# A fused attention and gated MLP block on one core: half-width GpSimd sums, a product sum built from PSUM alone, and weight words cut at other steps

## The chip, the cores and the metric

The kernel runs on one core of a Trainium2 chip. The metric is device time in microseconds (us) from launch to end; less is better. A measurement is the median of several runs; the profile is of one further execution with the hardware profiler on.

Engines are named as the profile names them: PE is TensorE's matmul, PEld its weight load, DVE is VectorE, ACT is ScalarE, POOL is GpSimd, SP is SyncE, which here only issues DMAs. Each engine works through its own queue in order, and waits at an instruction until the semaphores that it names have come.

## The reference

S = 2048 rows of D = 576 are normalized. One branch is linear attention with 32 heads, the other a gated MLP with Df = 4608; the result is x + s * silu(MLP). In the part that the change touches, all in float32:

```python
g = jnp.einsum("bsd,df->bsf", xn, w_gate)   # 2048x576 by 576x4608
u = jnp.einsum("bsd,df->bsf", xn, w_up)
h = _gelu(g) * u
mlp = jnp.einsum("bsf,fd->bsd", h, w_down)
```

## The kernel before

**Stages.** First attention's keys, values, queries and output, then (from 285 to 1123 us of the profile) the matrices of gate and up, last the down projection. The change lies in the third stage.

**Seven products instead of eight.** Each product of two matrices is cut into 2x2 blocks and computed with seven block products, from sums of blocks of X and of W. The stage runs 36 *matrices*, numbered q: q even is a gate, q odd the up matrix for the same 256 columns of Df (group g = q // 2 of NG = 18). A matrix has seven steps k, in each of which one word list of W meets one of X, for two halves s of the rows (s = 1 first):

```python
STEPS = (
    ("al", "A11", "B11"), ("ga", "S1", "T1"), ("de", "S3", "T3"), ("be", "S2", "T2"),
    ("al", "A12", "B21"), ("ga", "S4", "B22"), ("de", "A22", "T4"),
)
```

The first name is a pair of PSUM banks (one for each s). Steps 0 to 3 start banks, steps 4 to 6 accumulate into the banks of steps 0 to 2, and the next matrix takes the eight banks in rotation, so that each bank is taken up again four steps later. Between, its value must have been read; `step` in `matrix` (L882) says by whom.

**The matmuls.** A float32 operand is split into a high and a low float32r word, so a step has 27 matmuls of 32 rows by 512 columns for each s. TensorE is used as four groups of 32 rows, which run side by side, each some matmuls behind the one before it (`roll`, L828). All four are issued in one order: a matmul at the head that waits for a bank holds up all of them.

**The sum of products.** For each s, u holds al, the first product. The block C22 needs al + ga + de + be: ACT copies ga into a buffer (a gate uses the place in h where the result will be, an up matrix a temporary), DVE adds de, adds be to u, and adds u to the buffer. u, with be in it, then serves steps 5 and 6. A gate's four blocks pass through Gelu on ACT into h (`gate_matrix`, L911); an up matrix multiplies them into h on DVE (`up_matrix`, L934).

**Gated values.** The down projection is computed the same way, so at steps 5 and 6 of an up matrix POOL forms four sums and differences of blocks of h for each s (`hs`, 128x512), and SP stores h and hs: ten DMAs. For the last group DVE and POOL's DMA queue do it.

**Words of W.** `load_mat(q)` (L769) issues on SP the DMA of one matrix of W into `raw`, one buffer for even and odd alike. `mat_sums(q)` (L774) lets POOL form S1 to S4 from it into `sm`. `cut_w` (L786) cuts a block: ACT writes the high words, DVE two subtractions the low words, into `wa` (A11, S1, S3, S2) or `wb` (A12, A22, S4). `mat_pieces(q)` (L793) returns which of these cuts are made after which step of the matrix *before*: A11 after step 0, S1 and S3 after step 2, S2 after 3, A12 and A22 after 4, S4 after 6. `matrix_of(q)` (L1425) runs `mat_sums(q + 1)`, takes `mat_pieces(q + 1)` and adds to step 4 the load of matrix q + 2, which is allowed once A12 and A22 of q + 1 have been cut from `raw`. In a gate it also adds the load of a block of w_down (`td`) at step 0 and POOL's sums of it at step 3.

**Order.** All of this is pinned to program order, so the order in which the Python code calls `act`, `vec`, `pool` and `dma` is the order in each engine's queue. After the matmuls of a step and a half s follow the instructions of `step`; after the second half follow the pieces of that step.

Of the kernel before, what the change touches and what calls it, by code (L numbers as in the profile page):

```python
# [10 lines left out]
AF = mybir.ActivationFunctionType  # L11
# [4 lines left out]
P = 128  # L16
# [8 lines left out]
TBN = S // TB  # L25
TT = TBN // P
NG = DF // (2 * P)
# [38 lines left out]
def block_kernel(ctx, tc, x, xe, xt_d, wq_d, wkv0_d, wkv1_d, wkv2_d, wo, wgu_d, wd_d, out):  # L66
    nc = tc.nc
# [21 lines left out]
    def mid(i, shape, dt, name):  # L89
        return sb.tile(shape, dt, tag=f"m{i}", bufs=1, name=name)  # L90
# [7 lines left out]
    def tmp(shape, name):  # L98
        return sb.tile(shape, F32, tag="tmp", bufs=4, name=name)
# [3 lines left out]
    def act(*args, **kw):  # L103
        pin(nc.scalar.activation(*args, **kw))  # L104

    def vec(op, *args, **kw):
        pin(getattr(nc.vector, op)(*args, **kw))  # L107
# [6 lines left out]
    def pool(op, *args, **kw):  # L114
        pin(getattr(nc.gpsimd, op)(*args, **kw))  # L115

    def dma(out, in_, eng=None):
        tc.keep_in_program_order((eng or nc.sync).dma_start(out=out, in_=in_))
# [636 lines left out]
    raw, sums, wt = {}, {}, {}  # L755
# [30 lines left out]
    def cut_w(o, src, nm):  # L786

        r = group(W_LO[nm])
        act(o[:, :, 0:3, :], src, AF.Copy)
        vec("tensor_sub", o[:, :, 3:5, :], src[:, :, 0:2, :], o[:, :, 0:2, :].bitcast(F32))  # L790
        vec("tensor_sub", o[r, :, 2, :], src[r, :, 2, :], o[r, :, 2, :].bitcast(F32))

    def mat_pieces(q):  # L793

        if q >= NQ:
            return [[] for _ in range(7)]
        rv, sm = sums.pop(q)
        if q % 2 == 0:
            raws_ = [lambda: cut_w(wt["b"][:, 1:3], rv[:, 1], "A12")]
        else:  # L800
            raws_ = [
                lambda: cut_w(wt["b"][:, 1:2], rv[:, 1, 0:1], "A12"),
                lambda: cut_w(wt["b"][:, 0:1], rv[:, 1, 1:2], "A22"),
            ]
        return [
            [lambda: cut_w(wt["a"][:, 0:1], rv[:, 0, 0:1], "A11")],
            [],
            [lambda: cut_w(wt["a"][:, 1:3], sm[:, 0:2], "S1")],
            [lambda: cut_w(wt["a"][:, 3:4], sm[:, 2:3], "S2")],
            raws_,  # L810
            [],
            [lambda: cut_w(wt["b"][:, 3:4], sm[:, 3:4], "S4")],
        ]

    STEPS = (
        ("al", "A11", "B11"), ("ga", "S1", "T1"), ("de", "S3", "T3"), ("be", "S2", "T2"),
# [62 lines left out]
                        mats[q] = matrix_of(q)  # L879
                    mats[q](k, s, bs[q, bk, s])  # L880

    def matrix(q, c22, done, todo):  # L882

        u = {}

        def step(k, s, b):
            if k == 0:
                u[s] = tmp([P, TBN], f"u_{q}_{s}")
                act(u[s], b, AF.Copy)
            elif k == 1:  # L890
                act(c22(s), b, AF.Copy)
            elif k == 2:
                vec("tensor_add", c22(s), c22(s), b)
            elif k == 3:
                vec("tensor_add", u[s], u[s], b)
                vec("tensor_add", c22(s), c22(s), u[s])
                done(s, 1, 1, None)
            elif k == 4:
                done(s, 0, 0, b)
            elif k == 5:  # L900
                done(s, 0, 1, (u[s], b))
            else:
                done(s, 1, 0, (u[s], b))
            if s == SBS[-1]:
                run(todo[k])

        return step

    hid = {}

    def gate_matrix(g, todo):  # L911
        for s in SBS:
            for b in range(2):
                hid[s, b] = slot([P, 2, TBN], F32, f"h_{g}_{s}_{b}")

        def done(s, f, b, src):
            o = hid[s, b][:, f]
            if src is None:
                src = o
            elif isinstance(src, tuple):  # L920
                vec("tensor_add", o, *src)
                src = o
            act(o, src, AF.Gelu_apprx_tanh)

        return matrix(2 * g, lambda s: hid[s, 1][:, 1], done, todo)

# [5 lines left out]
    td_d = dr.tile([NG, P, 4, HALF], F32, name="td")  # L932

    def up_matrix(g, todo):  # L934
        c22, sm = {}, {}

        def take(s):
            if s not in c22:
                c22[s] = tmp([P, TBN], f"u22_{g}_{s}")
            return c22[s]  # L940

        def done(s, f, b, src):
            if src is None:
                src = c22[s]
            elif isinstance(src, tuple):
                o = src[0] if (f, b) == (1, 0) else tmp([P, TBN], f"u12_{g}_{s}")
                vec("tensor_add", o, *src)
                src = o
            h1, h2 = hid[s, 0], hid[s, 1]
            h = hid[s, b][:, f]  # L950
            vec("tensor_mul", h, h, src)
            d = hs_d[g][:, s]

            eng, sum_ = (nc.gpsimd, vec) if g == NG - 1 else (nc.sync, pool)
            if (f, b) == (0, 1):
                sm[s] = [gl_tile([P, TBN], f"hs_{g}_{s}_{i}") for i in range(3)]
                sum_("tensor_sub", sm[s][0], h1[:, 0], h2[:, 0])
                sum_("tensor_add", h2[:, 0], h2[:, 0], h2[:, 1])
                sum_("tensor_sub", sm[s][1], h2[:, 0], h1[:, 0])
                dma(out=d[:, 4], in_=sm[s][0], eng=eng)  # L960
                dma(out=d[:, 2:4], in_=h2, eng=eng)
            elif (f, b) == (1, 0):
                sum_("tensor_sub", sm[s][2], h1[:, 1], sm[s][1])
                dma(out=d[:, 0:2], in_=h1, eng=eng)
                dma(out=d[:, 5], in_=sm[s][1], eng=eng)
                dma(out=d[:, 6], in_=sm[s][2], eng=eng)

        return matrix(2 * g + 1, take, done, todo)

    td = {}  # L970

# [333 lines left out]
    for n in range(3, 2 * TT):  # L1305
# [8 lines left out]
        if TT <= n < 2 * TT - 1:  # L1314
            j, c = divmod(n - TT, 2)
# [98 lines left out]
    pieces = []  # L1414
# [3 lines left out]
            run(aside.get((tb, t), []))  # L1418
    wt["b"] = big(14, [P, 4, 5, P], F32R, "wb")
    back("T3")  # L1420
    run(pieces[4] + pieces[6])
    load_mat(1)
    back("B21", "B22", "T4", eng=nc.sync)

    def matrix_of(q):  # L1425

        g = q // 2
        mat_sums(q + 1)
        todo = mat_pieces(q + 1)
        if q % 2 == 0:  # L1430
            todo[0].append(lambda: load_down(g))
            todo[3].append(lambda: down_sums(g))
        todo[4].append(lambda: load_mat(q + 2))
# [69 lines left out]
```

## Time and profile before

| | us |
|---|---|
| median of three runs (1530.05, 1533.8, 1530.51) | 1530.51 |
| the profiled execution, whole | 1536.36 |
| its span, first to last instruction | 1534.6 |
| stage of gate and up matrices in it | 838 |
| one gate and one up matrix together (596.09 to 642.17) | 46.1 |
| busy in that pair: DVE | 35.9 |
| busy in that pair: POOL | 23.8 |
| busy in that pair: ACT | 15.4 |
| mean granted TensorE clock | 0.993 |

How to read the profile: the page's first part gives each engine's busy time. In the timeline a row has its start and length in us, the engine, the line of the helper that recorded it (L104 ACT, L107 DVE, L110 matmuls, L115 POOL, L118 DMAs), the operation, its tiles as out<-in with numbers left out, the form and count, and in brackets how long the engine stood idle before it and what ended that. Tile names carry the sense: `u<-al` is the copy of step 0, `wa<-raw` a cut of A11, `wa<-sm` of S1 and S3 or S2, `wb<-raw` of A12 and A22, `wb<-sm` of S4, `hs<-h` and `h<-h` on POOL the gated sums. A row of waits has who waited for whom, us in total, times, and the longest. Since the helpers have one line each, lines of code tell little here, tiles and times tell most.

### The profile page before, as it was taken

What the parts mean: (1) busy time and instruction counts of PE and PEld (TensorE: products, weight loads), DVE (VectorE), ACT (ScalarE), POOL (GpSimd) and SP (SyncE); (2) the same over time, 40 slices, a digit from 0 to 9 for tenths busy, and PEclk for the clock granted to TensorE, in tenths of its full rate; (3) what the DMA queues carried; (4) which work ended last, traced back from release to release, by engine and by line L of the source; (5) the groups of instructions that cost most, each with busy time, mean ns of one, the idle gap of its engine ahead of it and who ended that gap; (6) DMA issues with size and microseconds to landing.
All of it is one profiled execution on the core that took longest, in us unless ns stands there. A gap on an engine that the chain in (4) does not pass through costs nothing.

```text
span 1534.6 us, 42632 instructions
## 1 busy us (share of the span) xinstructions
PE 1489.4 (97%) x18431; PEld 1395.8 (91%) x18431; DVE 1074.2 (70%) x1651; ACT 614.6 (40%) x1155; POOL 548.0 (36%) x520
## 2 busy tenths in 40 slices
PE   9999999999999999999999999999999999999998
PEld 8989989998888988888988888988889999999998
DVE  7676567177788787788787787777684666555775
ACT  5444455233332333332333332333344545444543
POOL 5452521134655444655444655444510020000120
PEclk9999999899999999999999999999999999999999
DMA  6354015623443423443323443333687757787873
GB/s 231 128 217 165 1 52 193 247 79 129 169 170 135 148 100 129 170 169 134 150 99 129 170 170 134 139 110 129 221 285 246 253 167 251 245 267 246 281 243 127
DMA packets 114550, 261.98 MB, mean 171 GB/s; under 512 B 10218, under 2 KB 38634, under 8 KB 112314
## 3 DMA queue, kind: packets, MB, share of 16 engines
q1 hardware_dynamic: 112586, 249.95, 45.8%
q0 software_dynamic: 1632, 8.91, 1.6%
q8 instruction: 144, 2.36, 0.6%
q14 instruction: 44, 0.36, 0.1%
q10 hardware_dynamic: 144, 0.39, 0.1%
HBM read 161.27 MB, written 97.91 MB: 169 GB/s over the span
## 4 chain that ended last, share of the span: by engine, by line
PE 50%; issue 16%; DVE 14%; POOL 12%; DMA 4%; ACT 3%; POOLq 0%; ACTq 0%; SPq 0%; DVEq 0%
PE bd L1069 26%; PE kv L110 7%; POOL sm L115 5%; POOL hs L115 5%; DVE h L107 4%; PE de L110 4%; PE s L110 3%; DVE wa L107 3%; POOL h L115 3%; DVE u L107 3%; PE ga L110 3%; PE al L110 2%; DMA raw<-in_wgu_dram 2%; DVE wb L107 2%; PE q L110 2%
## 5 line engine op out<-in xcount | busy, mean ns | idle before, releaser
L1069 PE MATMUL bd<-t,s 128*128 128x288 f32 x3024 | 404.6, 296 | 2.4 <-DVE u L107 2.4
L1069 PEld LDWEIGHTS bd<-t,s 128*128 128x128 f32 x3024 | 403.8, 189 | 3.3 <-DVE u L107 2.9
L110 PE MATMUL al<-xo_B,wa 32*128 32x512 f32 x972 | 254.1, 394 | 14.3 <-DVE u L107 14.3
L107 DVE TENSOR_TENSOR s<-sr,s 128x512 fp32r<-128x512 f32 x252 | 176.0, 738 | 123.9 <-ACT s L104 120.2
L110 PE MATMUL ga<-xr_B,wb 32*128 32x512 f32 x972 | 253.5, 393 | 8.7 <-ACT h L104 8.6
L110 PE MATMUL ga<-xo_T,wa 32*128 32x512 f32 x972 | 253.8, 394 | 5.9 <-ACT h L104 5.9
L110 PE MATMUL de<-xo_T,wa 32*128 32x512 f32 x972 | 246.9, 389 | 5.5 <-DVE h L107 5.5
L110 PE MATMUL al<-xr_B,wb 32*128 32x512 f32 x972 | 252.1, 390 | 0.0
L110 PE MATMUL al<-xr_B,wa 32*128 32x512 f32 x972 | 251.7, 391 | 0.0
L110 PE MATMUL de<-xr_T,wb 32*128 32x512 f32 x972 | 250.5, 390 | 0.0
L110 PE MATMUL de<-xo_T,wb 32*128 32x512 f32 x972 | 249.1, 388 | 0.0
L110 PE MATMUL al<-xo_B,wb 32*128 32x512 f32 x972 | 247.0, 389 | 0.0
L110 PE MATMUL be<-xo_T,wa 32*128 32x512 f32 x972 | 246.8, 387 | 0.0
L110 PE MATMUL ga<-xr_T,wa 32*128 32x512 f32 x972 | 246.7, 389 | 0.0
L110 PE MATMUL ga<-xo_B,wb 32*128 32x512 f32 x972 | 244.5, 386 | 0.0
L110 PE MATMUL de<-xr_T,wa 32*128 32x512 f32 x972 | 244.0, 385 | 0.0
L110 PE MATMUL be<-xr_T,wa 32*128 32x512 f32 x972 | 243.9, 385 | 0.0
L104 ACT ACTIVATE s<-sr 128x512 fp32r<-128x512 f32 x252 | 149.0, 626 | 194.1 <-PE bd L1069 144.7
L110 PEld LDWEIGHTS al<-xo_B,wa 32*128 32x128 f32 x972 | 175.6, 185 | 24.9 <-DVE u L107 20.2
L110 PEld LDWEIGHTS ga<-xo_T,wa 32*128 32x128 f32 x972 | 177.4, 186 | 17.4 <-ACT h L104 12.5
L110 PEld LDWEIGHTS de<-xo_T,wa 32*128 32x128 f32 x972 | 177.8, 184 | 16.0 <-DVE h L107 11.8
L110 PEld LDWEIGHTS ga<-xr_B,wb 32*128 32x128 f32 x972 | 174.1, 184 | 19.3 <-ACT h L104 14.7
(177 smaller groups left out, 4351.5 us busy)
## 6 DMA issues: line engine op xcount, KB each, us to landing
sr<-hs SPq DMA_DIRECT2D x252, 256.0 KB
hs<-h SPq DMA_DIRECT2D x68, 512.0 KB
raw<-in_wgu_dram SPq DMA_DIRECT2D x36, 768.0 KB
hs<-hs SPq DMA_DIRECT2D x102, 256.0 KB
td<-in_wd_dram SPq DMA_DIRECT2D x18, 576.0 KB
td<-td SPq DMA_DIRECT2D x18, 576.0 KB
tr<-td SPq DMA_DIRECT2D x16, 576.0 KB
tr<-in_wd_dram SPq DMA_DIRECT2D x12, 576.0 KB
```

The lines of the kernel that those rows point to most:

```text
L104: pin(nc.scalar.activation(*args, **kw))
L107: pin(getattr(nc.vector, op)(*args, **kw))
L110: i = nc.tensor.matmul(*args, **kw)
L115: pin(getattr(nc.gpsimd, op)(*args, **kw))
L1069: nc.tensor.matmul(banks[j][:, 0:HALF], hw[n, s][:, a, t * P : (t + 1) * P], w[:, c, g % 4], start=(new and g == 0 and m == 0), stop=(g == ...
```

## The change

Four edits, all in the stage of gate and up matrices:

1. al + ga + de + be. ACT's copy of ga is gone. DVE writes a new temporary c22 = u + ga at step 1, adds de at step 2 and be at step 3 (then adds be to u as before). Three of the four additions read a PSUM bank; the addition of two SBUF buffers is gone. A gate's Gelu now reads c22 and writes h at step 3.
2. POOL's gated sums are made in two halves of 256 columns each.
3. The cuts move. For an up matrix (cut during a gate): A11 after step 0, then S1, S3 and S2 after step 3, A12 and A22 after 4, S4 after 5. For a gate (cut during an up matrix): A11 after 0, S1 and S3 after 2, S2 after 3, and A12, A22 and S4 after 6.
4. In an up matrix the load of matrix q + 2 moves from step 4 to step 6, behind the cuts of A12 and A22.

```diff
 def mat_pieces(q):
...
+        first = [lambda: cut_w(wt["a"][:, 0:1], rv[:, 0, 0:1], "A11")]
+        ones_ = [lambda: cut_w(wt["a"][:, 1:3], sm[:, 0:2], "S1")]
+        two = [lambda: cut_w(wt["a"][:, 3:4], sm[:, 2:3], "S2")]
+        four = [lambda: cut_w(wt["b"][:, 3:4], sm[:, 3:4], "S4")]
+        if q % 2:
+            return [first, [], [], ones_ + two, raws_, four, []]
+        return [first, [], ones_, two, [], [], raws_ + four]
...
 def matrix(q, done, todo):
...
             elif k == 1:
-                act(c22(s), b, AF.Copy)
+                c22[s] = tmp([P, TBN], f"c22_{q}_{s}")
+                vec("tensor_add", c22[s], u[s], b)
             elif k == 2:
-                vec("tensor_add", c22(s), c22(s), b)
+                vec("tensor_add", c22[s], c22[s], b)
             elif k == 3:
+                vec("tensor_add", c22[s], c22[s], b)
                 vec("tensor_add", u[s], u[s], b)
-                vec("tensor_add", c22(s), c22(s), u[s])
-                done(s, 1, 1, None)
+                done(s, 1, 1, c22[s])
...
 def up_matrix(g, todo):
...
-            eng, sum_ = (nc.gpsimd, vec) if g == NG - 1 else (nc.sync, pool)
+            eng = nc.gpsimd if g == NG - 1 else nc.sync
+
+            def sum_(op, o, a, b_):
+                if g == NG - 1:
+                    vec(op, o, a, b_)
+                    return
+                for c in (slice(0, TBN // 2), slice(TBN // 2, TBN)):
+                    pool(op, o[:, c], a[:, c], b_[:, c])
...
 def matrix_of(q):
...
-        todo[4].append(lambda: load_mat(q + 2))
+        todo[4 if q % 2 == 0 else 6].append(lambda: load_mat(q + 2))
```

The order on SP around the load of matrix 17, an up matrix, before; `hs_7` are the stores of group 7, `td_8` the block of w_down for group 8:

```order
L118 DMA raw_17_10214<-in_wgu_dram 128x1536
L118 DMA hs_7_86<-hs_7_1_0_10248 128x512
L118 DMA hs_7_86<-h_7_1_1_9498 128x1024
L118 DMA hs_7_86<-hs_7_0_0_10288 128x512
L118 DMA hs_7_86<-h_7_0_1_9500 128x1024
L118 DMA hs_7_86<-h_7_1_0_9497 128x1024
L118 DMA hs_7_86<-hs_7_1_1_10249 128x512
L118 DMA hs_7_86<-hs_7_1_2_10250 128x512
L118 DMA hs_7_86<-h_7_0_0_9499 128x1024
L118 DMA hs_7_86<-hs_7_0_1_10289 128x512
L118 DMA hs_7_86<-hs_7_0_2_10290 128x512
L118 DMA td_8_10443<-in_wd_dram 128x1152
```

And with the change:

```order
L118 DMA hs_7_86<-hs_7_1_0_10315 128x512
L118 DMA hs_7_86<-h_7_1_1_9568 128x1024
L118 DMA hs_7_86<-hs_7_0_0_10358 128x512
L118 DMA hs_7_86<-h_7_0_1_9570 128x1024
L118 DMA hs_7_86<-h_7_1_0_9567 128x1024
L118 DMA hs_7_86<-hs_7_1_1_10316 128x512
L118 DMA hs_7_86<-hs_7_1_2_10317 128x512
L118 DMA hs_7_86<-h_7_0_0_9569 128x1024
L118 DMA hs_7_86<-hs_7_0_1_10359 128x512
L118 DMA hs_7_86<-hs_7_0_2_10360 128x512
L118 DMA raw_17_10447<-in_wgu_dram 128x1536
L118 DMA td_8_10523<-in_wd_dram 128x1152
```

The load of matrix 17 moved from the head of the ten stores to behind them.

DVE around the first cut from that load, before: the end of up matrix 15 (`h_7_0_0`), S4 of matrix 16, A11 of matrix 17, and gate 16 (`h_8`, `u_16`) from its step 2 on.

```order
L107 TENSOR_TENSOR h_7_0_0_9499<-h_7_0_0_9499,u_15_0_9972 128x512
L107 TENSOR_TENSOR wb_3033<-sm_16_9936,wb_3033 128x256
L107 TENSOR_TENSOR wb_3033<-sm_16_9936,wb_3033 32x128
L107 TENSOR_TENSOR wa_2921<-raw_17_10214,wa_2921 128x256
L107 TENSOR_TENSOR wa_2921<-raw_17_10214,wa_2921 32x128
L107 TENSOR_TENSOR h_8_1_1_10404<-h_8_1_1_10404,de_16_1_10339 128x512
L107 TENSOR_TENSOR h_8_0_1_10406<-h_8_0_1_10406,de_16_0_10377 128x512
L107 TENSOR_TENSOR wa_2921<-sm_17_10398,wa_2921 128x2x256
L107 TENSOR_TENSOR wa_2921<-sm_17_10398,wa_2921 32x2x128
L107 TENSOR_TENSOR u_16_1_10407<-u_16_1_10407,be_16_1_10417 128x512
```

With the change:

```order
L107 TENSOR_TENSOR h_7_0_0_9569<-h_7_0_0_9569,u_15_0_10044 128x512
L107 TENSOR_TENSOR wb_3033<-raw_16_9850,wb_3033 128x2x256
L107 TENSOR_TENSOR wb_3033<-raw_16_9850,wb_3033 32x2x128
L107 TENSOR_TENSOR wb_3033<-sm_16_10008,wb_3033 128x256
L107 TENSOR_TENSOR wb_3033<-sm_16_10008,wb_3033 32x128
L107 TENSOR_TENSOR wa_2921<-raw_17_10447,wa_2921 128x256
L107 TENSOR_TENSOR wa_2921<-raw_17_10447,wa_2921 32x128
L107 TENSOR_TENSOR c22_16_1_10550<-u_16_1_10487,ga_16_1_10334 128x512
L107 TENSOR_TENSOR c22_16_0_10580<-u_16_0_10518,ga_16_0_10377 128x512
L107 TENSOR_TENSOR c22_16_1_10550<-c22_16_1_10550,de_16_1_10413 128x512
L107 TENSOR_TENSOR c22_16_0_10580<-c22_16_0_10580,de_16_0_10457 128x512
L107 TENSOR_TENSOR c22_16_1_10550<-c22_16_1_10550,be_16_1_10497 128x512
```

A12 and A22 of matrix 16 now stand ahead of A11 of matrix 17, behind A11 stand the reads of bank ga of gate 16, and S1 and S3 of matrix 17 come after be.

ACT at the same place with the change; after the copies of al comes A11's high word, and no copy of ga:

```order
L104 ACTIVATE u_16_1_10487<-al_16_1_10265 128x512
L104 ACTIVATE u_16_0_10518<-al_16_0_10295 128x512
L104 ACTIVATE wa_2921<-raw_17_10447 128x384
L104 ACTIVATE h_8_1_1_10484<-c22_16_1_10550 128x512
L104 ACTIVATE h_8_0_1_10486<-c22_16_0_10580 128x512
L104 ACTIVATE wa_2921<-sm_17_10478 128x2x384
```

Before, two copies of ga into h stood between A11 and S1 and S3.

More of the change, by code (lines that the diff above doesn't have):

```diff
@@ L804, in mat_pieces @@
             ]
[L805 to L813, printed above, removed]
+        first = [lambda: cut_w(wt["a"][:, 0:1], rv[:, 0, 0:1], "A11")]
[5 more added lines that the diff above has]
+        return [first, [], ones_, two, [], [], raws_ + four]
     STEPS = (
@@ L880, in roll, with matrix @@
                     mats[q](k, s, bs[q, bk, s])
-    def matrix(q, c22, done, todo):
-        u = {}
+    def matrix(q, done, todo):
+        u, c22 = {}, {}
         def step(k, s, b):
@@ L917, in done @@
             o = hid[s, b][:, f]
-            if src is None:
-                src = o
-            elif isinstance(src, tuple):
+            if isinstance(src, tuple):
                 vec("tensor_add", o, *src)
@@ L923, in done @@
             act(o, src, AF.Gelu_apprx_tanh)
-        return matrix(2 * g, lambda s: hid[s, 1][:, 1], done, todo)
+        return matrix(2 * g, done, todo)
     H_AT = {"A11": 0, "A12": 1, "S1": 2, "A22": 3, "S3": 4, "S2": 5, "S4": 6}
@@ L934, in up_matrix @@
     def up_matrix(g, todo):
[L935 to L940, printed above, removed]
+        sm = {}
         def done(s, f, b, src):
-            if src is None:
-                src = c22[s]
-            elif isinstance(src, tuple):
+            if isinstance(src, tuple):
                 o = src[0] if (f, b) == (1, 0) else tmp([P, TBN], f"u12_{g}_{s}")
@@ L966, in done @@
                 dma(out=d[:, 6], in_=sm[s][2], eng=eng)
-        return matrix(2 * g + 1, take, done, todo)
+        return matrix(2 * g + 1, done, todo)
     td = {}
@@ L1420, in block_kernel @@
     back("T3")
-    run(pieces[4] + pieces[6])
+    run(pieces[4] + pieces[5] + pieces[6])
     load_mat(1)
```

## The prediction

> **What bounds the kernel now.** I began with the page: its first part gives the span and each engine's busy time.
>
> ```profile
> span 1534.6 us, 42632 instructions
> PE 1489.4 (97%) x18431; PEld 1395.8 (91%) x18431; DVE 1074.2 (70%) x1651; ACT 614.6 (40%) x1155; POOL 548.0 (36%) x520
> ```
>
> TensorE is the bound, and what an edit on other engines can win or lose is idle time of TensorE. The change lies in the stage of gate and up matrices. The view of weight loads by tile bounds that stage (columns: count; ns; first and last start), and the view of waits, restricted to 300 to 1100 us, names who stops TensorE there.
>
> ```profile
> L110 PEld LDWEIGHTS al<-xo_B,wa x972: 180/183/333, 284.7 to 1102.8; 32*128 32x128 f32 x195
> L110 PEld LDWEIGHTS de<-xr_T,wb x972: 180/183/324, 309.1 to 1122.8; 32*128 32x128 f32 x195
> PE ga L110 <- ACT h L104: 14.5, 23, 2.0
> PE al L110 <- DVE u L107: 14.3, 14, 1.4
> PE de L110 <- DVE h L107: 5.1, 13, 0.6
> ```
>
> The stage takes 838 us for 36 matrices. Three waits come round once per gate, and all are for a PSUM bank that ACT or DVE reads late. The timeline shows the size of the loss. The first copies of one up matrix, the gate after it and the next up start at:
>
> ```profile
> 596.09 0.58 ACT L104 ACTIVATE u<-al 128x512 f32<-128x512 f32 x1
> 617.60 0.60 ACT L104 ACTIVATE u<-al 128x512 f32<-128x512 f32 x1 [4.11 <-PE al L110]
> 642.17 0.58 ACT L104 ACTIVATE u<-al 128x512 f32<-128x512 f32 x1
> ```
>
> The up matrix took 21.5 us, the gate 24.6, for the same number of matmuls: a gate loses about 3.1 us. Why, the timeline of DVE, ACT and POOL says:
>
> ```profile
> 610.51 1.29 DVE L107 TENSOR_TENSOR h<-h,al 128x512 f32<-128x512 f32 x2
> 611.71 1.12 DVE L107 TENSOR_TENSOR wb<-raw,wb 128x512 fp32r<-128x512 f32 x2
> 612.86 0.69 DVE L107 TENSOR_TENSOR u<-u,ga 128x512 f32<-128x512 f32 x1
> 614.36 1.29 POOL L115 TENSOR_TENSOR hs<-h,h 128x512 f32<-128x512 f32 x1 [13.02 <-DVE h L107]
> 619.53 2.81 DVE L107 TENSOR_TENSOR wb<-sm,wb 128x256 fp32r<-128x256 f32 x2
> 622.37 2.77 DVE L107 TENSOR_TENSOR wa<-raw,wa 128x256 fp32r<-128x256 f32 x2
> 623.51 2.79 POOL L115 TENSOR_TENSOR hs<-h,hs 128x512 f32<-128x512 f32 x2
> 624.95 0.60 ACT L104 ACTIVATE h<-ga 128x512 f32<-128x512 f32 x1 [3.76 <-DMA hs<-h]
> 628.27 0.85 ACT L104 ACTIVATE wa<-sm 128x768 fp32r<-128x768 f32 x1 [2.73 <-POOL sm L115]
> 629.15 1.84 DVE L107 TENSOR_TENSOR wa<-sm,wa 128x512 fp32r<-128x512 f32 x2 [2.70 <-ACT wa L104]
> 631.02 0.69 DVE L107 TENSOR_TENSOR u<-u,be 128x512 f32<-128x512 f32 x1
> ```
>
> At the start of a gate, POOL still sums the gated values of the up matrix before it (614.4 to 626.3), and four small DVE operations on two SBUF operands, which start one after another with POOL's, take 5.6 us. ACT stands at the copy into h until h has been stored. Then the S1 and S3 words wait for POOL's sums of W, and the addition of be, which frees the bank for the next matrix, stands behind them on DVE until 631.0.
>
> **What the change takes out.** Three parts aim at those rows. The copy of ga into h goes, and with it the 3.76 us wait for the stores; its replacement reads u and the bank into a buffer of its own. The words S1 and S3 of an up matrix come after both additions of be. And with A12 and A22 out of step 4 of the up matrix, the additions of step 5 follow the two h<-h,al at once: at 611.8, not 612.86, so POOL's sums start 1.1 us earlier, at 613.3. Additions cost DVE four more operations in two matrices, 4 x 0.69 = 2.8 us in 46.1; they fall at step 1, where the timeline has DVE waiting or in the four small operations, so I charge nothing, and 2.8 us per pair at most if that cover were gone. If every such wait goes, a gate takes the up matrix's 21.5 us: 3.0 us saved is what I take, 1.0 if only the largest part of one wait goes.
>
> **What it puts in the way.** A load of W may start only when the words of the matrix in the same buffer are cut. With A12 and A22 cut at step 6 of an up matrix, the load of the next up matrix moves to the end of step 6, and on the SP queue it stands behind all ten stores of gated values; before, it stood ahead of them. The last of those stores waits for POOL's last half sum. Its first reader is the word A11, in step 0 of the gate: on ACT the copy, and on DVE two subtractions, which stand directly ahead of the new additions c22<-u,ga of step 1. Step 5 of the same gate accumulates into the bank that these additions read, so TensorE stops there until the load has landed. That A11 itself is due only seven steps later does not help: both engines work in order. The rows for the price:
>
> ```profile
> 612.97 0.33 SPq L118 DMA_DIRECT2D raw<-in_wgu_dram  x1
> 627.38 1.36 SPq L118 DMA_DIRECT2D td<-in_wd_dram  x1
> 633.28 3.86 POOL L115 TENSOR_TENSOR td<-td 128x288 f32<-128x288 f32 x4 [2.56 <-DMA td<-in_wd_dram]
> 684.58 0.33 SPq L118 DMA_DIRECT2D raw<-in_wgu_dram  x1
> 689.31 1.99 POOL L115 TENSOR_TENSOR sm<-raw 128x384 f32<-128x384 f32 x2 [6.12 <-DMA raw<-in_wgu_dram]
> L115 POOL TENSOR_TENSOR wq<-rq,wq 128x256 fp32r<-128x256 f32 x4 | 3.0, 739 | 7.5 <-ACT wq L104 7.5
> 619.68 0.52 ACT L104 ACTIVATE wa<-raw 128x384 fp32r<-128x384 f32 x1
> 642.29 0.75 DVE L107 TENSOR_TENSOR wb<-sm,wb 128x256 fp32r<-128x256 f32 x2 [1.11 <-ACT wb L104]
> 644.73 1.74 DVE L107 TENSOR_TENSOR wa<-raw,wa 128x256 fp32r<-128x256 f32 x2 [1.68 <-ACT wa L104]
> 623.70 0.18 PEld L110 LDWEIGHTS ga<-xo_B,wb 32*128 32x128 f32 x1
> ```
>
> Step by step, on the clock of the gate at 617.6:
> - *POOL's sums.* Eight became sixteen of half the columns. One of 128x256 takes 0.74 us (row wq); with 0.08 us between two, 16 x 0.82 = 13.1 us. DVE's seven two-operand operations in that time (three products of h, two words of A12 and A22, two of S4; 0.3 to 0.7 us each, 3.9 together at most) push in between. Below: two halves cost what one whole did, and the sums take the 11.9 us of now (614.36 to 626.30). Above: 13.1 + 3.9 = 17.0. DVE's operations overlap POOL's start-up in the rows above (eight alone, at 1.29 and 0.08, would take 11.0, and with seven DVE operations took 11.9), so I take 14.6: end at 627.9.
> - *The load.* Now the load of td follows the stores: issued 1.1 us after POOL's last sum, used 5.9 us after its issue. A load of raw on a free queue is used 4.7 us after its issue (684.58 to 689.31). So 5.8 to 7.5 us from the last sum, the upper end because raw has 768 KB where td has 576; I take 6.6: landed at 634.5.
> - *The release.* 0.52 for ACT's copy, 1.74 for the two subtractions while POOL sums W beside them (as at 644.73), 0.69 for the addition, 0.15 for the hand-overs: 3.1 us; 2.1 if POOL were idle, when a pair of this shape takes 0.75 (642.29). Bank free at 637.6.
> - *The stop.* TensorE's first weight load of step 5 stood at 623.70. 637.6 - 623.7 = **13.9 us** per gate; 9.4 with all lower ends, 17.2 with all upper ones.
>
> A hole of that length also has a price when TensorE starts again. The two largest holes of this trace (PE's timeline, then stretches with weight loads, granted clock, DMA):
>
> ```profile
> 397.39 0.49 PE L110 MATMUL ga<-xr_B,wb 32*128 32x512 f32 x1 [1.99 <-ACT h L104]
> 397.40:400.80 3.40, 3.03 (x64) 1.00 0.86 299
> 904.03 0.49 PE L110 MATMUL ga<-xr_B,wb 32*128 32x512 f32 x1 [1.90 <-ACT h L104]
> 905.50:908.90 3.40, 2.76 (x32) 0.50 0.76 255
> 908.90:912.30 3.40, 2.99 (x60) 1.00 0.05 17
> ```
>
> After a hole of 2.0 us the granted clock stayed full; after one of 1.9 us it was 0.50 for 3.4 us, with 32 weight loads where the next stretch has 60: 28/60 x 3.4 = 1.6 us lost. A hole seven times as long should meet the second fate: 1.6 per gate, 0 to 3.2. The Trainium skill, "TensorE: Matmul & The Clock Gate", section "What's actually happening", states half clock after an idle window of about 3.4 us, and full clock after a busy one, with windows that run freely. By that rule a restart inside a window could cost the rest of it and a whole one, up to two of the row's prices; the sum would then be 27 us (17 x 1.6) longer. Both holes are shorter than the rule's window and one of them lowered the clock: as to when, the rows go before the rule.
>
> **The sum.** 17 loads are moved (after up matrices 1, 3 to 33; the first two are loaded ahead), so 17 gates stop: 17 x (13.9 + 1.6 - 3.0) = 17 x 12.5 = +212 us. The profiled execution took 1536.4 us (1534.6 and 1.8 around it), 5.9 above the median of 1530.5; so 1748 for such an execution and **1743 us** for the median. All lower ends: 17 x (9.4 - 3.0) = +109, 1640. All upper ends: 17 x (17.2 + 3.2 - 1.0) = +330, 1860. They won't all fall together; this case's own range is 1665 to 1815.
>
> **The rivals.** *The load is hidden, faster* (0.05): if ACT and DVE didn't stand at A11, only the saving remains, 17 x 3.0 = 51 us, 1480. For it: TensorE needs A11 a whole matrix later. Against it: in the order of both engines A11 precedes work that frees banks. It decides the sign wherever the load lands before 620.6 (623.7 less 3.1), that is when POOL's sums end by 614; they start at 613.3.
> *The halves shorten POOL's sums* (0.08): DVE waits for half an operation, gets through earlier, and the two engines lose less to each other; the sums end at 625.2 or before, the load takes its shortest and restarts are free: 1640 or less. For it: 5.6 us for four small operations now. Against: the 0.74 us row, more than half of 1.29. It is also the case in which halving does what it is for; in mine it only adds POOL time.
> *The clock stays down longer* (0.06). At the stage's entry the granted clock was halved for three times as long (stretches of weight loads):
>
> ```profile
> 287.70:297.90 10.20, 9.58 (x79) 0.50 1.00 401
> ```
>
> At 60 loads in 3.4 us these 79 need 4.5 us, so 5.7 are lost; with that at each restart the sum grows by 17 x 4.1 = 70, 1813. For it: a hole of 14 us is far longer than 1.9. Against: the entry fills TensorE slowly, the restart has its matmuls queued.
>
> **How the numbers follow.** My case 0.81, the rivals 0.05, 0.08 and 0.06. The range 1650 to 1815 leaves out the faster rival, most of the second and the tail of the third. About 0.3% (5 us) is what a measurement of this kernel tells from no change. Faster 0.05, the first rival; same 0.01; slower 0.94, all others.
>
> **What would show it.** In the trace after: PE's waits led by ga behind DVE c22, once per gate from the second on, 9 to 17 us each; ACT wa<-raw waiting for DMA raw in every gate; SP's raw after the last hs store; no wait of ACT h for DMA hs at step 1; granted clock below 1 once per pair; twice as many POOL sums hs and h, of 128x256, mean near 0.75 us; a gate of 34 to 38 us beside an up of 21.5. I am wrong if raw lands before TensorE reaches step 5, if DVE's c22 additions run ahead of A11, or if a gate is shorter than 24.6 us.

## The result, and the profile after

The changed kernel took 1734.51 us (median of four runs, 1730.35 to 1737.32) against 1530.71 for the kernel before on the same chip: a ratio of 1.1325, with a 95% interval of 1.1294 to 1.1356. The forecast was 1743 us in a range of 1650 to 1815, slower at 0.94.

The page of the changed kernel, its span and its first part, in the order PE, PEld, DVE, ACT, POOL; then the granted clock by slices:

```profile
span 1735.6 us, 42929 instructions
PE 1504.3 (87%) x18431; PEld 1423.5 (82%) x18431; DVE 1049.1 (60%) x1723; ACT 575.9 (33%) x1083; POOL 562.9 (32%) x656
PEclk9999999988898889888988898889889999999999
```

The matmuls are as many as before and TensorE is busy about as long (1504.3 us, 1489.4 before), but its share of the span fell from 97% to 87%. The span grew by 201 us, PE's busy time by 15: TensorE stands still, and the low digits of PEclk say where, in the slices of the gate and up matrices.

The view of waits between 300 and 1300 us (who waited for whom; us in total, times, longest) names one wait of TensorE, and another row what feeds it:

```profile
ACT wa L104 <- DMA raw<-in_wgu_dram: 241.9, 17, 15.0
PE ga L110 <- DVE c L107: 220.9, 17, 13.8
```

Seventeen times ACT stands at a cut of W until the load of raw has come, and seventeen times TensorE stands at bank ga behind DVE's addition c22 (tile c): 220.9 us in all, 13.0 each. The three waits of before, 14.5 + 14.3 + 5.1 us, are gone from this view.

One gate by the timeline (start, length, engine, line, operation; in brackets the idle time before and what ended it), POOL, then SP's queue, ACT, DVE and PE:

```profile
683.28 1.44 POOL L115 TENSOR_TENSOR hs<-h,h 128x256 f32<-128x256 f32 x2 [13.66 <-DVE h L107]
686.51 4.18 POOL L115 TENSOR_TENSOR hs<-h,h 128x256 f32<-128x256 f32 x4
693.85 2.78 POOL L115 TENSOR_TENSOR hs<-h,hs 128x256 f32<-128x256 f32 x4
696.17 1.78 SPq L118 DMA_DIRECT2D hs<-hs  x2
698.05 1.03 SPq L118 DMA_DIRECT2D raw<-in_wgu_dram  x1
688.13 0.60 ACT L104 ACTIVATE u<-al 128x512 f32<-128x512 f32 x1 [4.15 <-PE al L110]
703.98 0.52 ACT L104 ACTIVATE wa<-raw 128x384 fp32r<-128x384 f32 x1 [13.65 <-DMA raw<-in_wgu_dram]
724.49 0.60 ACT L104 ACTIVATE u<-al 128x512 f32<-128x512 f32 x1 [0.56 <-PE al L110]
704.53 1.80 DVE L107 TENSOR_TENSOR wa<-raw,wa 128x256 fp32r<-128x256 f32 x2 [11.93 <-ACT wa L104]
706.36 1.28 DVE L107 TENSOR_TENSOR c<-u,ga 128x512 f32<-128x512 f32 x2
707.10 0.79 PE L110 MATMUL ga<-xo_B,wb 32*128 32x512 f32 x1 [12.43 <-DVE c L107]
```

Read by time it is one chain. POOL's sums end at 696.63; SP, which has worked through the ten stores until then, issues the load of raw at 698.05; ACT's cut of A11 starts at 703.98, DVE's two subtractions at 704.53, the first addition that reads ga at 706.36, and TensorE takes the bank at 707.10. The gate lasts from 688.13 to 724.49, 36.4 us; that of before lasted 24.6.

By the windows view (first all engines: length, busy us and count of PE, PEld, DVE, ACT and POOL, granted clock, DMA share, GB/s; then weight loads alone) of that gate, the up matrix after it, and the stretches around the restart:

```profile
687.89:723.89 36.00, 23.57 (x380) 21.62 (x377) 18.13 (x29) 8.92 (x16) 16.71 (x20) 0.81 0.45 167
723.89:745.43 21.54, 21.54 (x384) 20.84 (x382) 16.19 (x26) 4.39 (x8) 7.93 (x10) 1.00 0.07 24
697.60:707.10 9.50, 0.00 (x0) 0.50 0.69 242
707.10:711.30 4.20, 3.35 (x44) 0.50 0.02 6
711.30:715.50 4.20, 3.79 (x76) 1.00 0.34 140
```

The up matrix is as it was. In the gate the clock falls during the hole (at 697.60, 2.9 us after TensorE stopped) and stays at 0.50 for 4.2 us after the restart, in which 44 weights are loaded where the next 4.2 us hold 76.

For means over the stage, a matrix is measured here and below from the last weight load of its step 0 (first half of rows) to the same load of the next matrix; over the 17 gates from the second on and the 17 up matrices ahead of them. Before, a gate took 24.52 us and an up matrix 21.58; after, 36.52 and 21.53. The difference, 17 x (12.00 - 0.05) = 203 us, is the whole of the 203.8 measured: nothing outside these gates matters.

### The profile page after: what moved, and what is told of

Read it like the earlier page. It is cut to its first block, busy times and chain, and to the rows that moved or that the text cites. A ratio compares the mean times of both kernels' runs of the same rounds, so it can differ in the third digit from the quotient of the medians.

```text
span 1735.6 us, 42929 instructions
## 1 busy us (share of the span) xinstructions
PE 1504.3 (87%) x18431; PEld 1423.5 (82%) x18431; DVE 1049.1 (60%) x1723; ACT 575.9 (33%) x1083; POOL 562.9 (32%) x656
## 4 chain that ended last, share of the span: by engine, by line
PE 70%; DVE 12%; DMA 7%; issue 4%; POOL 4%; SPq 2%; ACT 1%; POOLq 0%; ACTq 0%; DVEq 0%
PE bd L1067 23%; PE ga L110 13%; PE de L110 8%; PE al L110 8%; DMA raw<-in_wgu_dram 7%; PE kv L110 6%; DVE h L107 4%; PE be L110 3%; PE s L110 3%; DVE wb L107 3%; PE q L110 3%; POOL hs L115 3%; SPq L118 2%; DVE u L107 2%; DVE wa L107 1%
## 5 line engine op out<-in xcount | busy, mean ns | idle before, releaser
L110 PE MATMUL ga<-xo_B,wb 32*128 32x512 f32 x972 | 271.3, 417 | 220.9 <-DVE c L107 220.9
L110 PEld LDWEIGHTS ga<-xo_B,wb 32*128 32x128 f32 x972 | 193.8, 201 | 239.0 <-DVE c L107 228.1
L110 PE MATMUL be<-xr_T,wa 32*128 32x512 f32 x972 | 271.2, 417 | 0.0
L110 PE MATMUL al<-xo_B,wb 32*128 32x512 f32 x972 | 267.4, 409 | 0.0
L110 PE MATMUL al<-xr_B,wb 32*128 32x512 f32 x972 | 263.9, 409 | 0.0
L110 PE MATMUL be<-xo_T,wa 32*128 32x512 f32 x972 | 263.6, 409 | 0.0
L110 PE MATMUL de<-xr_T,wa 32*128 32x512 f32 x972 | 259.3, 399 | 0.0
L107 DVE TENSOR_TENSOR wa<-raw,wa 128x256 fp32r<-128x256 f32 x72 | 49.4, 687 | 290.2 <-ACT wa L104 289.7
L110 PEld LDWEIGHTS be<-xo_T,wa 32*128 32x128 f32 x972 | 193.6, 199 | 2.8
L110 PEld LDWEIGHTS al<-xr_B,wb 32*128 32x128 f32 x972 | 193.5, 199 | 2.8
```

The source lines that it names most:

```text
L110: i = nc.tensor.matmul(*args, **kw)
```

## The experiments

The theory was that the place of the load costs everything, by way of three queues: the load behind the stores on SP, the cut of A11 behind the load on ACT and DVE, the reads of bank ga behind the cut. The rivals were that part of the price is the new additions' or the half sums' own, or the clock's. Each experiment has its ratio to the kernel before, and its gate and up matrix measured as above.

### The changed kernel with the load where it was

Even matrices cut A12 and A22 after step 4 again (S4 stays at 6), and the load follows at once, ahead of the stores.

```diff
-        return [first, [], ones_, two, [], [], raws_ + four]
+        return [first, [], ones_, two, raws_, [], four]
...
-        todo[4 if q % 2 == 0 else 6].append(lambda: load_mat(q + 2))
+        todo[4].append(lambda: load_mat(q + 2))
```

> The changed kernel with one thing undone: A12 and A22 of a gate are cut after step 4 of the up matrix again, and the load of W stands at step 4 in every matrix, ahead of the stores of gated values. c22 from PSUM, half sums and the up matrices' words stay as changed. My theory (the late load alone makes the hole): no hole behind the load, gate 21.5 to 22.5 us, 1475 to 1500 us in all. Rival (half sums on POOL or four more additions on DVE are what costs): above 1530 us.

Measured: 1508.88 us, ratio 0.9858 [0.9842, 0.9875]; gate 21.33, up 23.24. With one cut and its load put back, the change is faster than the kernel before: their place alone is worth 226 us. But the time lies above the range that was expected, and the gain is 22 us and not the 51 of a saving of 3.0 per gate: the gate shows that saving (3.2 us), while the up matrix lost 1.7. The view of waits, SP's queue and ACT in an up matrix:

```profile
PE ga L110 <- DVE c L107: 20.5, 15, 3.2
616.05 0.44 SPq L118 DMA_DIRECT2D td<-in_wd_dram  x1
624.19 0.32 SPq L118 DMA_DIRECT2D td<-td  x1
624.62 0.37 SPq L118 DMA_DIRECT2D raw<-in_wgu_dram  x1
629.84 0.53 ACT L104 ACTIVATE wa<-raw 128x384 fp32r<-128x384 f32 x1 [1.67 <-DMA raw<-in_wgu_dram]
```

It looks like the same mechanism in small: the load of the next gate is issued 0.4 us behind the store of td, which waits for POOL's sums of td; ACT waits 1.67 us for the load at A11, and TensorE stops at bank ga, now in up matrices. The last three experiments test this.

### The late load alone

The kernel before, with the cuts of A12 and A22 and the load that are made during an up matrix moved from step 4 to step 6; nothing else.

```diff
+        four = [lambda: cut_w(wt["b"][:, 3:4], sm[:, 3:4], "S4")]
...
-            raws_,
+            raws_ if q % 2 else [],
             [],
-            [lambda: cut_w(wt["b"][:, 3:4], sm[:, 3:4], "S4")],
+            four if q % 2 else raws_ + four,
...
-        todo[4].append(lambda: load_mat(q + 2))
+        todo[4 if q % 2 == 0 else 6].append(lambda: load_mat(q + 2))
```

> The kernel before with one part of the change: A12 and A22 of a gate cut after step 6 of the up matrix and the load behind them, no other part. My theory: the hole comes with this part alone; ACT's copy of ga stands behind A11 there, whole sums end 1 to 2 us earlier, a stop of about 10 us per gate, 1640 to 1720 us. Rival (it needs the additions of c22 behind A11 on DVE, or the half sums): within 1% of 1530 us.

Measured: 1682.93 us, 1.0993 [1.0971, 1.1015]; gate 33.47, up 21.56. By itself the move costs 152 us, three quarters of the whole. The wait is the same, by another reader of bank ga (waits, then ACT's timeline in a gate):

```profile
PE ga L110 <- ACT h L104: 169.7, 17, 10.9
626.31 0.52 ACT L104 ACTIVATE wa<-raw 128x384 fp32r<-128x384 f32 x1 [13.04 <-DMA raw<-in_wgu_dram]
626.74 1.07 ACT L104 ACTIVATE h<-ga 128x512 f32<-128x512 f32 x2
```

ACT's copy of ga into h starts 0.43 us after the start of the cut, without waiting for DVE's subtractions, so the bank is free some 2 us sooner after the landing than in the changed kernel: on the mean of 17 gates, 1.06 us pass from the start of the cut to TensorE's restart, 3.11 there.

### The changed kernel with whole sums

POOL's gated sums are made whole again, all else as changed.

```diff
-                for c in (slice(0, TBN // 2), slice(TBN // 2, TBN)):
-                    pool(op, o[:, c], a[:, c], b_[:, c])
+                pool(op, o, a, b_)
```

> The changed kernel with POOL's gated sums whole again, all else as changed. If the halves only lengthen the sums ahead of the load (13.3 us there, 11.9 for whole sums), the load lands 1.4 us earlier in each of 17 gates: 1734.5 - 24 = 1705 to 1718 us. If the clock's windows set the length of a pair (17 windows of 3.413 us are 58.03 us, the pair's measured mean), it falls by nothing or by a whole window, to 1735 or about 1677 us.

Measured: 1712.62 us, 1.119 [1.1174, 1.1206]; gate 35.22, up 21.53. The half sums cost 22 us of the 204. Waits, and the first and the last row of POOL's sums in one gate:

```profile
PE ga L110 <- DVE c L107: 195.1, 17, 12.4
674.00 1.30 POOL L115 TENSOR_TENSOR hs<-h,h 128x512 f32<-128x512 f32 x1 [13.61 <-DVE h L107]
683.50 2.75 POOL L115 TENSOR_TENSOR hs<-h,hs 128x512 f32<-128x512 f32 x2
```

Eight whole sums take 12.25 us, sixteen halves 13.35 (683.28 to 696.63): 1.1 us, and the gate is 1.3 us shorter. With this kernel and the one ahead of it, the 12.0 us by which a gate grew can be split, edit upon edit in this order: 24.52 to 33.47 by the place of the load (9.0), to 35.22 by the additions and the other words (1.8), to 36.52 by the halves (1.3).

### The late load on another queue

The load stays at step 6 of an up matrix, but ACT issues it.

```diff
-    def load_mat(q):
+    def load_mat(q, eng=None):
...
-            dma(out=raw[q], in_=wgu_d[q // 2, q % 2])
+            dma(out=raw[q], in_=wgu_d[q // 2, q % 2], eng=eng)
...
-        todo[4 if q % 2 == 0 else 6].append(lambda: load_mat(q + 2))
+        if q % 2 == 0:
+            todo[4].append(lambda: load_mat(q + 2))
+        else:
+            todo[6].append(lambda: load_mat(q + 2, nc.scalar))
```

> The changed kernel, but the load that moved to step 6 is issued from ACT's queue, so that it waits for the cut of A12 and A22 alone and not for the ten stores and POOL's sums. My theory (queue order behind the stores is the larger part of the hole): the cut ends 3.1 us into the gate, the load lands 8 to 9 us into it instead of 16, and TensorE's stop shrinks from 13 to 5 or 6 us per gate; 1570 to 1640 us. Rival (six words cut on DVE while POOL holds the shared port are the cause): as the changed kernel, about 1735 us.

Measured: 1597.28 us, 1.0433 [1.0411, 1.0456]; gate 28.41, up 21.54. ACT's timeline:

```profile
590.90 0.33 ACTq L118 DMA_DIRECT2D raw<-in_wgu_dram  x1
595.50 0.52 ACT L104 ACTIVATE wa<-raw 128x384 fp32r<-128x384 f32 x1 [3.13 <-DMA raw<-in_wgu_dram]
```

The load is used 4.6 us after its issue while POOL still sums and SP still stores. So 137 of the 204 us come back when the load no longer stands behind the stores on SP, at the same late step: TensorE's wait at ga fell to 67.1 us in 17. The rest of the distance to the kernel with the load put back, 88 us, is 7.1 us per gate less the 1.7 per up matrix that only that kernel loses. It is the later step, with a part that this way of issuing adds (ACT waits there for DVE's last read of raw, and TensorE for a bank al that ACT reads late: 10.2 us in 17); how much each is was not measured.

### The first reader placed later

A11 of an up matrix is cut after step 3 of the gate instead of step 0, so that no read of a bank of steps 1 to 3 stands behind it.

```diff
-            return [first, [], [], ones_ + two, raws_, four, []]
+            return [[], [], [], first + ones_ + two, raws_, four, []]
```

> The changed kernel with the load as late as in it, but A11 of an up matrix cut after step 3 with S1, S3 and S2 instead of after step 0. My theory (the hole is as long as it is because A11 stands ahead of the reads of bank ga): the stop at step 5 behind DVE c22 goes; ACT now waits for the load at step 3 and reads bank al late, a stop of 5 to 6 us at step 1 of the next matrix; 1555 to 1640 us. Rival (the late load costs the same wherever its first reader stands): about 1735 us.

Measured: 1613.4 us, 1.0539 [1.0517, 1.056]; gate 29.26, up 21.75. Waits, and ACT's cut of A11:

```profile
PE al L110 <- ACT wa L104: 72.1, 17, 4.9
608.44 0.52 ACT L104 ACTIVATE wa<-raw 128x384 fp32r<-128x384 f32 x1 [4.91 <-DMA raw<-in_wgu_dram]
```

The stop at ga is gone and 121 of the 204 us with it: the in-order stand of the bank's readers behind A11 is what turned the late load into a stop within the same gate. The place of what remains was not the one expected: TensorE waits for the word A11 itself, at step 0 of the next matrix. The cut starts 16.5 us after the gate's first copy (591.92 to 608.44), as soon as the load has landed, and DVE's subtractions, and POOL's sums of W with the cuts of S1 to S3, all come only then. The 121 us of this kernel and the 137 of the one before can't be added up: they break the same chain at two places.

### The other edits by themselves

Each is put into the kernel before by itself: first the additions from PSUM, then the half sums, then the changed kernel's order of the words that are cut in gates (code cut at the three dots):

```diff
-                act(c22(s), b, AF.Copy)
+                c22[s] = tmp([P, TBN], f"c22_{q}_{s}")
+                vec("tensor_add", c22[s], u[s], b)
...
             elif k == 3:
+                vec("tensor_add", c22[s], c22[s], b)
                 vec("tensor_add", u[s], u[s], b)
-                vec("tensor_add", c22(s), c22(s), u[s])
-                done(s, 1, 1, None)
+                done(s, 1, 1, c22[s])
```

> The kernel before with c22 built from PSUM banks alone, nothing else of the change (whole sums, cuts and load as before). My theory: ACT's wait for the stores goes, but the new reads of bank ga stand on DVE behind the four small operations that end 7.8 us into the gate; TensorE stops at step 5 for about 2 us instead of at al; no gain, 1515 to 1545 us. Rival (the copy behind the stores was the gate's loss): 1480 to 1500 us.

```diff
...
+                for c in (slice(0, TBN // 2), slice(TBN // 2, TBN)):
+                    pool(op, o[:, c], a[:, c], b_[:, c])
...
```

> The kernel before with POOL's gated sums in halves, nothing else. My theory: the four small DVE operations shrink from 5.6 us to some 3.4, but the sums end 1 to 2 us later, and ACT's copy into h and the cut of S1 and S3 wait for them; slower, 1540 to 1575 us. Rival (the port waits on DVE are the gate's loss): 1490 to 1515 us.

```diff
+        if q % 2:
+            return [
+                [lambda: cut_w(wt["a"][:, 0:1], rv[:, 0, 0:1], "A11")], [], [],
+                [lambda: cut_w(wt["a"][:, 1:3], sm[:, 0:2], "S1"),
+                 lambda: cut_w(wt["a"][:, 3:4], sm[:, 2:3], "S2")],
+                raws_, [lambda: cut_w(wt["b"][:, 3:4], sm[:, 3:4], "S4")], [],
+            ]
```

> The kernel before with the words of up matrices alone moved: S1 and S3 after step 3, S4 after step 5; A12 and A22 and the load as before. My theory: the addition of be no longer waits for POOL's sums of W, the stop at al goes, the wait of ACT's copy for the stores stays; 1490 to 1515 us. Rival (the stop only moves to bank ga): within 0.5% of 1530 us.

| edit alone | us | ratio | gate | up |
|---|---|---|---|---|
| additions from PSUM | 1510.83 | 0.9865 [0.985, 0.9879] | 23.37 | 21.54 |
| half sums | 1547.28 | 1.0104 [1.0091, 1.0117] | 25.47 | 21.58 |
| order of words in gates | 1518.33 | 0.9912 [0.9899, 0.9925] | 23.36 | 21.78 |

TensorE's waits in the stage: all of the first kernel, the largest of the second, all of the third:

```profile
PE ga L110 <- DVE c L107: 21.7, 17, 1.3
```

```profile
PE ga L110 <- ACT h L104: 29.2, 33, 2.4
```

```profile
PE de L110 <- DVE h L107: 18.1, 17, 1.5
PE ga L110 <- ACT h L104: 7.0, 8, 1.7
```

The additions saved more than was expected, since one wait of 1.3 us at ga took the place of all three. The order of words saved less: its wait at al went, and one of about the same size came at de. The half sums alone make the kernel slower: where ACT's copy into h still has to wait for POOL's sums to be stored, longer sums lengthen its wait (ga 29.2 us here, 14.5 before).

### The load put back, with whole sums

The first experiment's kernel with POOL's sums whole.

```diff
-                for c in (slice(0, TBN // 2), slice(TBN // 2, TBN)):
-                    pool(op, o[:, c], a[:, c], b_[:, c])
+                pool(op, o, a, b_)
```

> The version with the load ahead (1508.9 us) with POOL's gated sums whole again. My theory: with c22 on DVE the four small operations stand ahead of the reads of bank ga, and whole sums hold them to 7.8 us into the gate where halves let them end at 4.8: a stop of about 2 us per gate, 1525 to 1550 us. Rival (halves only lengthen the sums): 1495 to 1505 us.

Measured: 1509.16 us, 0.9863 [0.9848, 0.9879]; gate 23.21, up 21.75: the same time as with halves, where 1525 at least was expected. Not because halves do nothing. DVE's four small operations at the start of a gate of this kernel with the additions behind them, and the same four of the kernel with halves:

```profile
612.33 2.81 DVE L107 TENSOR_TENSOR wb<-sm,wb 128x256 fp32r<-128x256 f32 x2
615.17 2.76 DVE L107 TENSOR_TENSOR wa<-raw,wa 128x256 fp32r<-128x256 f32 x2
617.97 1.28 DVE L107 TENSOR_TENSOR c<-u,ga 128x512 f32<-128x512 f32 x2
```

```profile
605.76 1.71 DVE L107 TENSOR_TENSOR wb<-sm,wb 128x256 fp32r<-128x256 f32 x2
607.50 1.60 DVE L107 TENSOR_TENSOR wa<-raw,wa 128x256 fp32r<-128x256 f32 x2
```

Halves take the four from 5.6 to 3.3 us, so c22 reads bank ga sooner, and the gate gains 1.9 us. The up matrix gives 1.5 back: the next load is issued 1.6 us ahead of its first copy with halves, 5.0 with whole sums (means). About 0.9 us of that is POOL, which is done with h later, and so with td, whose store stands ahead of the load; the larger part is the shorter gate itself, which lets the up matrix begin 2.5 us earlier (from first copy to first copy).

### Taking the second stop out

Three more kernels start from the first experiment's. In one, A11 of a gate is cut after step 1, behind the reads of ga, instead of step 0.

```diff
-        return [first, [], ones_, two, raws_, [], four]
+        return [[], first, ones_, two, raws_, [], four]
...
-        (1, 0): [lambda: pieces.extend(first_matrix()), lambda: run(pieces[0])],
+        (1, 0): [lambda: pieces.extend(first_matrix()), lambda: run(pieces[0] + pieces[1])],
```

The second pair of lines only keeps A11 of the first matrix where it was.

> The version with the load ahead (1508.9 us), and A11 of a gate cut after step 1 of the up matrix instead of after step 0, so that the additions c22 = u + ga stand ahead of it. My theory (what is left there is the same mechanism in small: the gates' load, issued behind the store of td, holds A11 and with it the reads of bank ga): no wait of ga for DVE c22, up matrices back to 21.5 us, 1475 to 1495 us. Rival (DVE has too little time in the up matrix): within 0.5% of 1509 us.

Measured: 1488.84 us, 0.9725 [0.9712, 0.9739]; gate 21.32, up 22.00. TensorE's stop behind c22 is gone; its waits for a bank in the stage are 2.2 us at ga, behind DVE's additions into h, and 0.4 at al. Why an up matrix still takes 0.5 us more than 21.5 stays open. In the next, POOL's sums of td and their store come behind the load instead of ahead of it.

```diff
-            todo[3].append(lambda: down_sums(g))
-        todo[4].append(lambda: load_mat(q + 2))
+        todo[4].append(lambda: load_mat(q + 2))
+        if q % 2 == 0:
+            todo[4].append(lambda: down_sums(g))
```

> The version with the load ahead (1508.9 us), and POOL's sums of td, with their store, after step 4 of a gate behind the load of W instead of after step 3 ahead of it; A11 stays after step 0. My theory (the load is late because the store of td stands before it on SP): the load is issued 2 to 3 us earlier, ACT's wait of 37 us for it goes, 1475 to 1497 us. Rival (the cut of A12 and A22 sets the load's time): within 0.5% of 1509 us.

Measured: 1479.4 us, 0.9662 [0.9649, 0.9675]; gate 21.34, up 21.56. SP's queue shows the turned order:

```profile
604.66 0.75 SPq L118 DMA_DIRECT2D td<-in_wd_dram  x1
611.17 0.33 SPq L118 DMA_DIRECT2D raw<-in_wgu_dram  x1
613.57 0.33 SPq L118 DMA_DIRECT2D td<-td  x1
```

The load follows 6.5 us after that of td, 8.6 in the first experiment, and TensorE's only wait for a bank in the stage is one of 0.2 us. Last, both edits together.

> Both edits on the version with the load ahead: A11 of a gate after step 1, and the store of td behind the load. Each alone removes the same stop, so together no more than the better one: 1472 to 1492 us. Rival (two separate stops): 1460 us or less is out of reach, since 36 matrices at 21.5 us leave 1472 us.

Measured: 1478.26 us, 0.9655 [0.9641, 0.9668]; gate 21.31, up 21.54. This is the fastest of all, though its interval and that of the one before it overlap. Its page:

```profile
span 1476.1 us, 42961 instructions
PE 1463.5 (99%) x18431; PEld 1439.5 (98%) x18431; DVE 1042.5 (71%) x1723; ACT 572.2 (39%) x1083; POOL 558.4 (38%) x656
```

No wait of TensorE's matmuls is left in the stage of gate and up matrices. Whether whole sums would do as well here was not tried.

## Why the prediction was right

**The mechanism** held at each link: the load behind ten stores, POOL's last half sum ahead of the last store, A11 on ACT and DVE behind the load, c22 behind A11, and TensorE at step 5, once in each of 17 gates. Put the load back and the loss is gone; take the queue alone away and 137 us go; take A11 from ahead of the bank's readers and 121 go. What was to be seen in the trace was seen: 17 waits at ga, the longest 13.8 us, ACT's wait for raw 17 times, raw behind the last store of hs, no wait for the stores at step 1, a gate of 36.5 us beside an up matrix of 21.5.

**The terms**, against the gate at 688.13, with the means of the 17 gates. POOL's sums were taken as 14.6 us and took 13.35; they started 4.85 us ahead of the copy instead of 4.3, so that they ended 8.5 us after it and not 10.3. That is the same in every gate, and 1.8 us less than forecast. From the last sum to the cut of A11 it was 7.35 us here and 7.9 on the mean (6.9 to 8.7), not 6.6: 1.3 us more, and beyond the 7.5 that the forecast had for its upper end. On the mean, 1.3 us of it go by until the load is issued, 1.1 by forecast, and 6.6 from there to the cut. So the cut stood at +16.4 on the mean, forecast +16.9, and that it came so near is in part luck: two errors cancelled. The release was taken as 3.1 and was 3.1 (703.98 to 707.10). So the stop, 13.9 by forecast, was 13.4 on the mean of the 17 gates: the start of step 5 moved by that much against an up matrix's place. (TensorE's idle time before it, 13.0, is a little less.) The restart is the rest of the gate, 36.52 - 21.53 - 13.4 = 1.6, as taken, although the clock stayed at 0.50 for 4.1 us after it on the mean, not 3.4. And 17 x 0.5 = 8.5 us is what the forecast of 1743 was too high.

**Half sums.** Their mean was to be near 0.75 us and is not. By tile and shape (columns: busy us, mean ns of one, idle before):

```profile
L115 POOL TENSOR_TENSOR hs<-h,h 128x256 f32<-128x256 f32 x136 | 120.6, 912 | 229.2 <-DVE h L107 229.2
L115 POOL TENSOR_TENSOR hs<-h,hs 128x256 f32<-128x256 f32 x68 | 47.2, 722 | 0.0
```

Those that run alone, at the end, take 0.72 us, the price of the row that was used, but they follow each other every 0.70 us (2.78 for four at 693.85), not every 0.82: sixteen of them alone would take 11.1 us by that estimate, not 13.1. Those that alternate with DVE take longer, 4.18 us for four at 686.51. The forecast put DVE's share at up to 3.9 us and took about 1.5; of the 13.35 us it was some 2.2. Here, too, two errors go opposite ways: the sums by themselves were taken 2.0 us too long, DVE's share 0.7 too short.

**The saving** of 3.0 us per gate was right in size, but the changed kernel can't show it by itself: the hole covers all other waits. Without the hole, 22 us are saved and not 51, because the next stop in line, the load behind the store of td, takes its place; the 1480 us of the faster rival needed the order of that store turned as well (1479.4). Charging nothing for DVE's four additions was right in the up matrix, 21.53 us with them. Their price lay elsewhere: the release of bank ga moved from ACT to DVE, behind two subtractions. From the cut to the restart that is 2.05 us more (1.06 to 3.11), and POOL's sums end 0.4 us sooner; the gate grew by 1.8, from 33.47 to 35.22.

**The rivals.** The hidden load fell with the first row of ACT's wait for raw. The halves do speed up DVE's small operations (5.6 to 3.3 us where the load is put back), but POOL's sums, which set the time here, get longer by 1.1 us: without halves the changed kernel is 22 us faster, so this rival had the wrong sign for this order. The clock did not stay down longer: the restart cost 1.6 us and not the 5.7 that the entry of the stage suggested.

## What to carry to other kernels

A load on an in-order queue is as late as the latest producer of any store ahead of it, so a load that a due date depends on goes ahead of stores whose values are still being computed, or on another queue; the same holds for a small store (td here) as for ten large ones. Look not only at when a loaded word is due, but at what stands behind its first reader on each engine: here a word needed seven steps later stopped TensorE, because readers of PSUM banks stood behind its cut. And an edit that shortens one wait should be priced together with the wait that is next in line, for alone it gets only the distance between the two.

## What the runs showed of the hardware

The granted clock moved on a fixed grid. Three stretches of weight loads that follow each other in the changed kernel (us, weight loads busy, granted clock, DMA share, GB/s):

```profile
639.60:653.20 13.60, 2.61 (x36) 0.50 0.45 152
653.20:697.60 44.40, 40.80 (x724) 1.00 0.25 95
697.60:711.30 13.70, 3.35 (x44) 0.50 0.48 170
```

Each of the 17 holes, of whatever start, gave one stretch at half clock of 13.6 to 13.7 us, and the stretches began 58 us apart (639.60, 697.60, 755.60), while single pairs of matrices took 57.4 to 58.6. The clock fell 2.9 to 3.9 us after TensorE had stopped, and stayed low for 3.2 to 5.0 us beyond each restart. The Trainium skill, "TensorE: Matmul & The Clock Gate", section "What's actually happening", has a free-running window of 3413 ns; the trace agrees: four windows are 13.65 us and seventeen 58.0. In the other kernels with a hole the stretches were 3.4, 6.8, 10.2 or 13.7 us long, one to four times 3.41. The grid did not set the time of a pair: POOL's 1.1 us moved the gate by 1.3.

A short hole had no smaller price at its end than a long one. With the first reader placed later, TensorE's holes were 4.2 us long on the mean, and the half clock still ran for 4.8 us beyond the restart, 4.1 in the changed kernel with its holes of 13.0. At 609.02 TensorE took up work again, and in the 6.8 us at 0.50 from 608.10 on it loaded 60 weights, 108 in the next 6.8.

DVE and POOL hold each other up. A product of h by u, two SBUF operands, took 0.69 us before POOL began and 1.2 while POOL summed (start, length):

```profile
682.51 0.69 DVE L107 TENSOR_TENSOR h<-h,u 128x512 f32<-128x512 f32 x1
687.74 1.21 DVE L107 TENSOR_TENSOR h<-h,u 128x512 f32<-128x512 f32 x1
685.19 0.67 DVE L107 TENSOR_TENSOR u<-u,de 128x512 f32<-128x512 f32 x1
```

The addition that reads PSUM kept its 0.67 us between them. The Trainium skill, "SBUF — State Buffer", section "Who interferes with whom", says that a VectorE instruction with two SBUF inputs contends with a GpSimd instruction that reads SBUF, and that one with at most one SBUF input, outside the modes that use two ports, does not; these rows agree. The four small operations take the longer the longer POOL's instructions are (2.8 us a pair beside whole sums, 1.6 to 1.7 beside halves).
